# Top-k attention and a SoLU block in one kernel: score buffers over half of the keys for two heads, two query loads per step, and a new order

## The chip, the cores and the metric

The kernel runs on one core of one Trainium2 chip. The metric is the device time of one execution in microseconds. Before the change it is 1203.38 us, the median of three runs (1203.36 to 1203.61). Engines are named as in the profile: PE (TensorE), DVE (VectorE), ACT (ScalarE), POOL (GpSimd), and SP, which here issues all loads and stores.

## The reference

q, k and v have shape (8, 8, 576, 64): batch, heads, sequence, head size, in float32. The second block has float64 weights of 512 x 1024 and 1024 x 512.

```python
scores = scale * np.matmul(q, k.transpose(0, 1, 3, 2))
kth = np.partition(scores, -top_k, axis=-1)[..., -top_k:-top_k + 1]   # top_k = 32
scores = np.where(scores >= kth, scores, -1000000000.0)
scores = scores - np.max(scores, axis=-1, keepdims=True)
attn = np.exp(scores)
attn = attn / (np.sum(attn, axis=-1, keepdims=True) + 1e-09)
x = np.matmul(attn, v)            # then (B,H,S,D) -> (B*S, H*D): 4608 x 512
...
h = x @ w_in
e = np.exp(h - np.max(h, axis=-1, keepdims=True))
solu = h * (e / (np.sum(e, axis=-1, keepdims=True) + 1e-09))
ln = (solu - mean) / np.sqrt(var + 1e-06) * g_ln
out = ln @ w_out
```

So each query keeps its 32 largest of 576 scores, takes a softmax over them, and the result goes through two matrix products with a gate and a layer norm between them.

## The kernel before

**Tiling.** 576 queries are four blocks of 128 and a tail of 64. The work is in 32 *steps*, four for each batch: a step takes two pairs of heads and two blocks of queries of each, which makes four chunks of 128 queries x 2 heads, and a fifth chunk with the two tails of one pair. A score row block is called j: j = 2t and 2t+1 are the two heads of chunk t, j = 8 is the tail chunk. Steps 2n and 2n+1 of a batch together give the attention output of two blocks of 128 tokens for all heads; these are *tokens* (36 groups of 128 rows), and the second block runs once for each: mm1 (x w_in), hexp, solu, square, spread, ln, transpose_ln, mm2 (x w_out), store, send.

**A step.** SP loads q (load_q, L2125, four loads, one for each chunk) and, for each pair of heads, k, the tails of q and k, and v (load_k, load_t, load_v). PE turns them (prep_q, prep_k, prep_t; the rows tp_qk and pre); ACT copies them out and squares them. PE makes an estimate of each row's score size (estimate, the rows est), DVE's length and POOL's root turn it into a first threshold, which begin (L2184) puts into t0. PE then multiplies queries by keys: scores (L2202) handles one chunk t at a time. It takes two PSUM buffers `big` of 2 x 512 words, one for each head, with keys 0 to 287 in the first half and 288 to 575 in the second. A head has 64 rows, so the two heads use the upper and the lower half of the PE array, and their products stand alternately in the queue. ACT's evac (L2221) scales one buffer into X in SBUF, DVE counts how many of its scores pass t0 (count0, the rows junkv; two to four of the nine on ACT), moves the threshold by the count (second, moved, even), ACT counts again with signs (count1, the rows sg), DVE picks the values nearest to the threshold (nearest, best: the MAX8 rows), merges them into the exact 32nd value (merged, which, chosen, kth), and keeps the exponentials above it (keep, the rows E). PE turns these (transpose_p, transpose_last), ACT copies them into PT (copy_p), PE multiplies them by v (attn_v, attn_t, the rows om), and DVE's copy_v divides by the sums into xTm or xTt, which are the tokens' input.

**The weights.** Sixteen chunks of 512 KB are loaded as float64 (load_w), cut to float32 by DVE (w_bits, w_corr), added up on PE (w_sum) and copied by ACT (w_copy). mm1 needs all of w_in, so the first eight must be through. At the end they are loaded again and looked at (w_again, w_exp, w_check).

**Order.** All engines but SP follow an order written out by a planner. work_of lists each operation with its engine, an assumed duration, what it comes after, and which buffers it uses; PLACES holds one number, a due date, for each operation; arranged (L698) goes through time, and on each engine it takes, of the operations that can start soonest (within PATIENCE of the soonest, L1777), the one with the smallest place. SP's loads are issued in this order too. PE uses its array in three forms, the full one (`f`), by row halves (`r`, scores) and by column halves (`c`, attn_v), and the plan books a price for each change of form. Buffers that matter here: two `big` (scores, and mm1's result for a whole token), two `o` (estimates, attention outputs, mm2's results, turned tails), two `tp` (transposes), eight X.

Of the kernel before, what the change touches and what calls it, by code (L numbers as in the profile page):

```python
# [15 lines left out]
P = 128  # L16
# [426 lines left out]
class Work:  # L443
# [18 lines left out]
    "ends", "keep", "ln", "key_stats", "w_bits", "w_corr", "w_gain",  # L462
# [31 lines left out]
def work_of(B, NP, steps, NF, w_wide):  # L494
# [15 lines left out]
    for b in range(B):  # L510
        for hp in range(NP):
            n = pair(b, hp)
            add(("load_k", n), "SP", 1350, behind("load_k", n), [("km", n)], late=2300)
            add(("load_t", n), "SP", 1650, behind("load_t", n), [("qkt", n)], late=3000)
            add(("load_v", n), "SP", 1650, behind("load_v", n), [("vm", n), (f"vd{n % 4}", n)], late=3000)
# [9 lines left out]
    for i, (b, chunks) in enumerate(steps):  # L525
# [3 lines left out]
        add(("load_q", i), "SP", 2200, behind("load_q", i), [("q", i)], late=2400)  # L529
# [10 lines left out]
        add(("begin", i), "DVE", 80, [("root", i)], [("o", ("est", i)), ("small", i)], 80)  # L540
        turned = [("transpose_last", i - 1, u) for u in range(2)] if i else []
        turned += [("transpose_p", i - 1, j) for j in range(NT)] if i else []
        for t in range(NM + 1):
# [6 lines left out]
            add(("scores", i, t), "PE", 970, ready + [("scores", i - 1, u) for u in before],  # L550
                [("big", (i, j)) for j in js] + x + [("kT", n)] + ([("qT", i)] if t < NM else []),
                mode="r" if t < NM else "f")
            for j in js:
                add(("evac", i, j), "ACT", 531, [("scores", i, t)], [("big", (i, j)), ("small", i)] + x, 110)
                on_a = j >= NT - few_of(i)
                add(("count0", i, j), "ACT" if on_a else "DVE", 770 if on_a else 737,
                    [("begin", i), ("evac", i, j)], x + [("small", i)], 110 if on_a else 82)
# [103 lines left out]
    for n in range(NW):  # L661
        if w_wide:
            tag = ("X", ("w", n)) if 2 <= n < 6 else ("E", ("w", n)) if 6 <= n < 10 else ("lnT", ("w", n))
            add(("load_w", n), "SP", 2700, behind("load_w", n), [tag], 3500)
# [33 lines left out]
def arranged(work, rank):  # L698
# [23 lines left out]
    while len(start) < len(ops):  # L722
# [56 lines left out]
        -231922, -235093, -18042, -259815, 53881, -26910, 98693, 89295, 121016, 46316, 230106,  # L779
        355121, 274522, 360371, 391010, 446355, 444309, 504026, 537837, 507457, 575009, 582585,  # L780
        750366, 671489, 709965, 699022, 831359, 799848, 825482, 840407, 964227, 982302,
    ],
    "load_t": [
        -247901, -201100, -260957, 23891, 20177, 142488, 125581, 104238, 96313, 290803, 250948,
        316178, 307259, 403270, 342301, 413782, 396239, 494754, 589937, 526814, 579905, 664149,
        686757, 657519, 760755, 797410, 777584, 782250, 759984, 828408, 986254, 1052144,
    ],
    "load_v": [
        4513, -28316, 65834, 70032, 237412, 276299, 189136, 198676, 274775, 314238, 308304,
        315468, 396251, 396215, 501580, 466234, 545375, 599484, 587563, 603323, 638479, 756008,  # L790
        748529, 764396, 836844, 775398, 911922, 867656, 992809, 1068251, 1042268, 1092371,
    ],
    "prep_t": [
        -66024, -35218, -106968, -124979, 106380, 92968, 113423, 124982, 186474, 259308, 243381,
        264175, 349208, 365073, 403353, 423445, 427516, 433224, 489877, 478123, 625612, 662465,
        677716, 720421, 790096, 792821, 833195, 820447, 902635, 952541, 903717, 984623,
    ],
    "prep_tc": [
        -3659, 6982, 125129, 194480, 58479, 110962, 16603, 132387, 247838, 253849, 255570, 364359,
        401263, 437048, 412216, 468592, 538576, 465027, 572960, 574254, 624893, 670844, 740941,  # L800
        688304, 822521, 772593, 803972, 799637, 876671, 914493, 987945, 1053957,
    ],
    "prep_k": [
        -66034, -37947, -116787, -114223, 61830, 112826, 44679, 124730, 221869, 282666, 218678,
        312796, 373609, 360416, 374756, 444621, 506839, 560741, 514149, 602405, 665351, 668819,
        660569, 737807, 783550, 770963, 815648, 854771, 921629, 983616, 926036, 997868,
    ],
    "prep_kc": [
        -31830, 34481, -43910, 188250, 14844, 72034, 129236, 181508, 247818, 306656, 255884,
        418155, 369635, 416315, 460884, 487557, 508176, 499093, 549171, 549826, 679307, 654196,  # L810
        730255, 740546, 813255, 656582, 761008, 847058, 1011512, 968974, 1021267, 1014780,
    ],
    "key_square": [
        -6107, 9200, -18931, 213036, 67709, 48480, 69177, 125029, 263257, 285990, 199299, 423686,
        366563, 422347, 432668, 464275, 526013, 529993, 663289, 617129, 615223, 689260, 733195,
        763121, 824760, 755412, 803556, 820850, 972811, 973391, 963453, 1065640,
    ],
    "tail_square": [
        -9398, -37371, 24328, 181845, 66940, 136814, 56754, 125050, 274345, 247045, 271022,
        361521, 313475, 423910, 396880, 417393, 448163, 489613, 561645, 544046, 671031, 673625,  # L820
        718576, 687624, 812310, 696685, 804699, 833105, 852776, 972218, 965549, 1038215,
    ],
    "key_stats": [
        49244, 90323, 131224, 7666, 155042, 84463, 99397, 97289, 253693, 307081, 241289, 211979,
        339462, 399467, 402326, 455602, 486238, 511354, 589917, 612160, 565404, 712946, 729447,
        715533, 757814, 727456, 817143, 897941, 916106, 958459, 945063, 1071720,
    ],
    "load_q": [
        -203866, 57324, 47623, 69971, -30777, -6747, 92399, 81781, 190840, 208167, 261724, 303295,
        302878, 366925, 467745, 502581, 494867, 437968, 460600, 600618, 608413, 668795, 680197,  # L830
        761552, 682102, 671226, 845894, 865571, 874423, 860434, 1017679, 975249,
    ],
    "prep_q": [
        -79677, -117866, 32032, 13411, 86950, 135549, 225889, 127973, 183269, 276392, 244143,
        336055, 374788, 314311, 427218, 502907, 575463, 550697, 484754, 603196, 662484, 708755,
        710771, 750650, 762039, 831240, 855758, 847165, 910722, 955644, 1037349, 1050639,
    ],
    "prep_qc": [
        -2082, 188201, 134073, 119961, 51146, 125087, 198593, 145727, 249393, 219238, 284776,
        340139, 381991, 373070, 445301, 406892, 528101, 558348, 560625, 609324, 613546, 702436,  # L840
        680953, 773525, 758549, 795279, 864443, 884402, 902803, 974600, 1007236, 1087201,
    ],
    "query_square": [
        48602, 219690, 10502, 204666, 77178, 115847, 200979, 184149, 259522, 249591, 359749,
        338859, 430728, 461236, 461439, 480399, 516251, 557645, 605853, 636513, 639337, 685605,
        695232, 779265, 734075, 807377, 902692, 935429, 938819, 975439, 1117707, 1080921,
    ],
    "estimate": [
        -51721, 24520, 32537, 42039, 32686, 43251, 188650, 175963, 183605, 293926, 314412, 304383,
        406485, 355203, 465841, 523950, 454436, 555291, 600732, 655321, 676831, 585411, 743542,  # L850
        767341, 797214, 877957, 887133, 892412, 966830, 1025698, 881531, 1005532,
    ],
    "length": [
        13505, 24395, 62143, 74804, 27409, 136316, 213529, 202175, 282027, 342718, 372938, 330157,
        492709, 436992, 478114, 487587, 493364, 622122, 589139, 617588, 678258, 747400, 748131,
        761353, 821982, 912838, 922484, 921913, 987763, 1030027, 1037987, 1090530,
    ],
    "root": [
        119641, 113709, 124208, 125050, 115227, 123468, 183009, 143050, 342821, 318954, 283414,
        288875, 476686, 507680, 494982, 529348, 539265, 557472, 575475, 651531, 750654, 756244,  # L860
        740467, 755497, 809920, 900416, 886522, 961896, 980436, 1024386, 979437, 1047371,
    ],
    "begin": [
        -11098, -32177, 114058, 97689, 127135, 163126, 183911, 238625, 258237, 332322, 343785,
        337307, 443545, 446760, 512382, 463995, 468265, 527542, 611248, 597194, 702846, 746359,
        777678, 796090, 780698, 866074, 840375, 898381, 996092, 1006714, 1032142, 1052602,
    ],
    "scores": [
        [-66043, -32432, -117187, -55548, -58649],
        [32509, -86744, -84674, 14425, -118098],  # L870
        [-1709, 59539, 206, 62497, 1680],
        [97632, 36717, 37420, 110204, 21187],
        [126461, 66992, 95602, 22391, 180659],
        [225092, 132274, 170298, 187038, 132279],
        [221524, 185438, 98417, 149447, 208257],
        [235554, 234327, 205686, 276399, 197567],
        [274165, 278537, 273676, 258560, 301244],
        [278510, 351700, 329880, 301926, 326114],
        [326121, 301381, 291542, 293719, 437364],
        [320084, 368685, 363929, 372753, 342271],  # L880
        [363314, 353920, 356109, 316998, 390713],
        [283384, 427244, 513881, 447027, 282054],
        [589195, 496452, 535821, 356932, 465873],
        [517528, 510229, 487313, 458650, 439441],
        [553852, 547378, 551693, 443165, 441345],
        [564875, 622931, 590176, 557220, 582546],
# [1854 lines left out]
```

## Time and profile before

| What | us |
|---|---|
| Median of three runs | 1203.38 |
| The profiled execution, its own time | 1203.71 |
| Its span, first to last instruction | 1201.9 |
| PE busy, mean granted clock 0.982 | 1147.5 |
| s_ps, row-half products (1024 rows, 512 products) | 170.1 busy |
| h_ps and o_ps, products with w_in and w_out | 229.2 + 28.9 and 257.9 busy |
| sg on ACT, second counts | 196.5 busy |
| root on POOL (zs, 32 times) | 1.976 each |

One product in float32 appears as two rows in the profile, a transpose as one. Times are starts and durations from the span's beginning; ends on PE are modelled, so the distance from one start to the next says more than a duration. The profile's page gives the engines' totals and a strip of 40 slices of 30 us each, in tenths. The timeline merges rows of one kind that follow each other, with the idle time before them and what ended it in brackets.

### The profile page before, as it was taken

Reading aid. Unit: us, or ns where it says so; the run is one execution under the profiler, and the core shown is the slowest. Engines: PE = TensorE matmul, PEld = TensorE weight load, DVE = VectorE, ACT = ScalarE, POOL = GpSimd, SP = SyncE. Lnnn points to the kernel's source line nnn. Section 1 sums busy time; section 2 is a strip of 40 time slices with the busy share of each in tenths; the row PEclk is TensorE's granted clock in tenths of the full one; section 3 lists DMA queues with packets and bytes.
Section 4 is the critical chain, followed back from the end, with each engine's and each line's share of the span. In section 5 each row is a group of like instructions: output and inputs, shape, how many; then the busy total and the mean of one; then the engine's idle time right before and its main releaser. Section 6 shows DMA issues by size and latency. Waiting matters only on the chain.

```text
span 1201.9 us, 18981 instructions
## 1 busy us (share of the span) xinstructions
PE 1147.5 (95%) x5866; PEld 661.0 (55%) x5868; DVE 1047.0 (87%) x3113; ACT 1011.2 (84%) x2180; POOL 149.9 (12%) x167
## 2 busy tenths in 40 slices
PE   6676999999999999999999999999999999999997
PEld 3354555555655655565565555555555556555553
DVE  5899899999888998999989888999898888999910
ACT  7789779989987998999896999899887899888642
POOL 1100020202022020210012020211113001110110
PEclk9689899999999999999999999999999999999999
DMA  6312201111110211120120211111120011122501
GB/s 174 113 53 71 88 21 52 35 31 42 58 47 18 60 43 56 30 69 24 39 66 10 52 44 51 49 36 46 31 74 28 25 28 41 57 71 90 177 19 30
DMA packets 111433, 64.56 MB, mean 54 GB/s; under 512 B 90445, under 2 KB 98906, under 8 KB 111322
## 3 DMA queue, kind: packets, MB, share of 16 engines
q1 hardware_dynamic: 111322, 63.25, 18.8%
q8 instruction: 49, 0.80, 0.3%
q14 instruction: 62, 0.51, 0.1%
HBM read 53.65 MB, written 9.57 MB: 53 GB/s over the span
## 4 chain that ended last, share of the span: by engine, by line
PE 58%; DVE 23%; ACT 14%; issue 2%; POOL 1%; DMA 1%; SPq 0%; DVEq 0%; ACTq 0%
PE o_ps L2625 16%; PE h_ps L2564 11%; PE s_ps L2214 10%; PE tp_p L2467 7%; PE om L2523 7%; DVE junkv L2231 5%; ACT sg L2288 4%; DVE w L2320 4%; DVE w L2309 4%; DVE E L2390 4%; ACT E L2345 2%; PE tp_ln L2614 2%; PE tp_qk L2087 2%; PE om L2532 2%; ACT PT L2480 2%
## 5 line engine op out<-in xcount | busy, mean ns | idle before, releaser
L2625 PE MATMUL o_ps<-w_out,lnT 128*128 128x512 f32 x576 | 257.9, 593 | 0.1
L2564 PE MATMUL h_ps<-w_in,xTm 128*128 128x512 f32 x512 | 229.2, 594 | 0.0
L2320 DVE MAX8 w<-w 128x8 f32<-128x288 f32 x576 | 224.1, 446 | 0.3
L2288 ACT ACTIVATE sg<-X,t 128x576 bf16<-128x576 f32 x256 | 196.5, 778 | 12.6 <-DVE t L2273 12.1
L2309 DVE SCALAR_TENSOR_TENSOR w<-X,al,sg 128x576 f32<-128x576 f32 x256 | 202.0, 815 | 0.9
L2390 DVE SCALAR_TENSOR_TENSOR E<-X,kth,E 128x576 f32<-128x576 f32 x256 | 198.6, 816 | 2.3 <-ACT E L2345 1.1
L2223 ACT ACTIVATE X<-s_ps 128x576 f32<-128x576 f32 x256 | 159.1, 664 | 41.9 <-PE s_ps L2214 41.1
L2231 DVE TENSOR_SCALAR_CACHE_REDUCE junkv<-X,t 128x576 bf16<-128x576 f32 x216 | 174.4, 807 | 13.4 <-ACT X L2223 7.0
L2214 PE MATMUL s_ps<-kT,qT 64*128 64x288 f32 x1024 | 170.1, 440 | 1.6 <-ACT X L2223 0.8
L2467 PE MATMUL tp_p<-ident,E 128*128 128x128 f32 x1024 | 151.3, 279 | 17.8 <-ACT PT L2480 6.2
L2625 PEld LDWEIGHTS o_ps<-w_out,lnT 128*128 128x128 f32 x576 | 105.1, 190 | 111.1 <-issue 110.3
L2480 ACT COPY PT<-tp_p 128x512 f32<-128x512 f32 x256 | 148.0, 598 | 13.1 <-PE tp_p L2467 12.8
L2467 PEld LDWEIGHTS tp_p<-ident,E 128*128 128x128 f32 x1024 | 116.0, 141 | 77.8 <-issue 29.9
L2345 ACT ACTIVATE E<-X 128x1152 f32<-128x1152 f32 x128 | 149.6, 1187 | 0.9 <-PE tp_p L2467 0.9
L2564 PEld LDWEIGHTS h_ps<-w_in,xTm 128*128 128x128 f32 x512 | 93.3, 190 | 98.4 <-issue 96.3
L2523 PE MATMUL om<-PT,vm 128*64 128x256 f32 (+1 forms) x1024 | 138.5, 415 | 2.5 <-ACT PT L2480 1.5
L2182 POOL TENSOR_TENSOR zs<-zs,phalf 128x9 f32<-128x9 f32 x32 | 63.2, 1976 | 507.2 <-DVE zs L2175 500.0
L2214 PEld LDWEIGHTS s_ps<-kT,qT 64*128 64x128 f32 x1024 | 96.7, 191 | 52.8 <-issue 24.2
L2523 PEld LDWEIGHTS om<-PT,vm 128*64 128x64 f32 x1024 | 69.5, 138 | 58.5 <-issue 10.4
L2599 POOL TENSOR_SCALAR var<-var 128x1 f32<-128x1 f32 x36 | 12.7, 354 | 514.3 <-ACT e_sb L2593 514.2
L2593 ACT ACTIVATE e_sb<-solu,nmu 128x1024 f32<-128x1024 f32 x36 | 41.5, 1152 | 14.8 <-DVE nmu L2587 14.6
L2575 ACT ACTIVATE e_sb<-h_ps 128x1024 f32<-128x1024 f32 x36 | 36.7, 1020 | 19.9 <-PE h_ps L2564 19.8
(144 smaller groups left out, 1506.9 us busy)
## 6 DMA issues: line engine op xcount, KB each, us to landing
km<-in_k_dram SPq DMA_DIRECT2D x32, 256.0 KB
q_sb<-in_q_dram SPq DMA_DIRECT2D x128, 64.0 KB
vm<-in_v_dram SPq DMA_DIRECT2D x32, 256.0 KB
out_dram<-osb SPq DMA_DIRECT2D x32, 256.0 KB
scales<-rows SPq DMA_DIRECT2D x58, 128.0 KB
w_raw<-in_moe_w_in_dram SPq DMA_DIRECT2D x8, 512.0 KB
w_raw<-in_moe_w_out_dram SPq DMA_DIRECT2D x8, 512.0 KB
w_again<-in_moe_w_in_dram SPq DMA_DIRECT2D x8, 512.0 KB
```

The costliest lines, as they stand in the source:

```text
L2214: nc.tensor.matmul(out=big[h][:, half, 0:SH], lhsT=queries_of(i, t)[hd, :], rhs=kT[hd, k0 : k0 + SH], start=True, stop=True,)
L2231: nc.vector.tensor_scalar(out=junk, in0=x_of(i, j), scalar1=st[i][t][:, j : j + 1], scalar2=None, op0=ALU.is_ge, op1=ALU.add, accum_out=co ...
L2288: nc.scalar.activation(out=d["sg", j], in_=x_of(i, j), func=AF.Sign, scale=-(1.0 + 2.0**-23), bias=d["t1"][:, j : j + 1], accum_out=column ...
L2309: nc.vector.scalar_tensor_tensor(out=w, in0=x_of(i, j), scalar=d["al"][:, j : j + 1], in1=d.pop(("sg", j)), op0=ALU.subtract, op1=ALU.mult,)
L2320: nc.vector.max(w8[:, j, 8 * half : 8 * half + 8], w[:, half * SH : (half + 1) * SH])
L2345: nc.scalar.activation(out=d["E", t], in_=d["X", t], func=AF.Exp)
L2390: nc.vector.scalar_tensor_tensor(out=e, in0=x_of(i, j), scalar=d["kth"][:, j : j + 1], in1=e, op0=ALU.is_ge, op1=ALU.mult, accum_out=den_a ...
L2467: nc.tensor.transpose(tp[:, c, :], e[:, c * P : (c + 1) * P], ident)
L2480: nc.scalar.copy(out=dst, in_=st[i].pop(("tp", j)))
L2523: nc.tensor.matmul(out=o[h * D : (h + 1) * D, cols], lhsT=vm[:, h, c, :], rhs=pt[:, h * NM + c, :], start=(c == 0), stop=False,)
L2564: nc.tensor.matmul(out=h[:, half, :], lhsT=x[:, c, :], rhs=w_in[:, c, half * 512 : (half + 1) * 512], start=(c == 0), stop=(c == NP - 1),)
L2625: nc.tensor.matmul(out=o, lhsT=d["lnT"][:, c, :], rhs=w_out[:, c, :], start=(c == 0), stop=(c == NF - 1),)
```

## The change

1. **Scores by halves of the keys.** The operation is now scores(i, j). For chunk t it takes one buffer `big`; the first 512 words hold head 0 and the second 512 words head 1, both for the same 288 keys. j = 2t is the first half of the keys, 2t+1 the second. evac writes the two heads' parts into the two rows' places in X. A first count of a head now comes after both evictions of its chunk. The tail chunk stays as it was.
2. **Queries in two loads.** A step's four chunks are two neighbouring pairs of heads at two neighbouring blocks, so one load fetches four heads of one block. The tile's axes change, and the turning picks its four parts from it.
3. **Estimates leave PSUM at once.** length scales both halves of the estimate with a constant tile `parts` into SBUF; begin adds them from there and no longer holds the estimate's PSUM buffer.
4. **ranks** is one row of 16 constants, read by broadcast over the nine j.
5. **The plan.** Other assumed durations for loads, PATIENCE above zero, and new PLACES for all operations.

```diff
-            add(("load_k", n), "SP", 1350, behind("load_k", n), [("km", n)], late=2300)
-            add(("load_t", n), "SP", 1650, behind("load_t", n), [("qkt", n)], late=3000)
+            add(("load_k", n), "SP", 950, behind("load_k", n), [("km", n)], late=2300)
+            add(("load_t", n), "SP", 1800, behind("load_t", n), [("qkt", n)], late=2100)
...
-        add(("begin", i), "DVE", 80, [("root", i)], [("o", ("est", i)), ("small", i)], 80)
+        add(("begin", i), "DVE", 80, [("root", i)], [("small", i)], 80)
...
-            add(("scores", i, t), "PE", 970, ready + [("scores", i - 1, u) for u in before],
-                [("big", (i, j)) for j in js] + x + [("kT", n)] + ([("qT", i)] if t < NM else []),
-                mode="r" if t < NM else "f")
             for j in js:
-                add(("evac", i, j), "ACT", 531, [("scores", i, t)], [("big", (i, j)), ("small", i)] + x, 110)
+                add(("scores", i, j), "PE", 485 if t < NM else 970,
+                    ready + [("scores", i - 1, u) for u in range(NT if i else 0)],
+                    [("big", (i, j))] + x + [("kT", n)] + ([("qT", i)] if t < NM else []),
+                    mode="r" if t < NM else "f")
+                add(("evac", i, j), "ACT", 531, [("scores", i, j)], [("big", (i, j)), ("small", i)] + x, 110)
+            for j in js:
                 on_a = j >= NT - few_of(i)
                 add(("count0", i, j), "ACT" if on_a else "DVE", 770 if on_a else 737,
-                    [("begin", i), ("evac", i, j)], x + [("small", i)], 110 if on_a else 82)
+                    [("begin", i)] + [("evac", i, u) for u in js], x + [("small", i)], 110 if on_a else 82)
...
-PATIENCE = {"PE": 0, "ACT": 0, "DVE": 0, "POOL": 0, "SP": 0}
+PATIENCE = {"PE": 300, "ACT": 100, "DVE": 100, "POOL": 100, "SP": 2000}
...
     def load_q(i):
         b, chunks = steps[i]
-        qt = st[i]["q"] = p2.tile([P, 2 * NM, D], F32, tag="q", name="q_sb")
-        for c, (hp, t) in enumerate(chunks):
-            nc.sync.dma_start(
-                out=qt[:, 2 * c : 2 * c + 2, :],
-                in_=q[b, 2 * hp : 2 * hp + 2, 0:SM, :].rearrange("h (p t) d -> p t h d", t=NM)[
-                    :, t, :, :
-                ],
-            )
+        first, t = min(chunks)
+        qt = st[i]["q"] = p2.tile([P, 2, NM, D], F32, tag="q", name="q_sb")
+        rows = q[b, 2 * first : 2 * first + NM, 0:SM, :].rearrange("h (p t) d -> p t h d", t=NM)
+        for n in range(2):
+            nc.sync.dma_start(out=qt[:, n, :, :], in_=rows[:, t + n, :, :])
...
     def length(i):
-        zs = st[i]["zs"] = small.tile([P, NT], F32, tag="zs", name="zs")
-        nc.vector.tensor_scalar(
-            out=zs, in0=st[i]["est"][:, 0, 0:NT], scalar1=(Z0 * scale) ** 2 / SM, scalar2=None,
-            op0=ALU.mult,
-        )
+        both = st[i]["both"] = small.tile([P, 2, NT], F32, tag="zs", name="zs")
+        st[i]["zs"] = both[:, 0, :]
+        nc.vector.tensor_tensor(
+            out=both, in0=st[i]["est"][:, :, 0:NT], in1=parts, op=ALU.mult
+        )
...
-    def scores(i, t):
+    def scores(i, j):
         d = st[i]
+        t, k = divmod(j, 2)
         kT = keys_of(i, t)["kT"]
-        js = [2 * t] if t == NM else [2 * t, 2 * t + 1]
-        big = [ps_big.tile([P, 2, 512], F32, tag="big", name="s_ps") for _ in js]
-        for half in range(2):
-            for h in range(len(js)):
-                hd = slice(0, P) if t == NM else slice(h * D, (h + 1) * D)
-                k0 = half * SH + (ST if h == 0 else 0)
-                nc.tensor.matmul(
-                    out=big[h][:, half, 0:SH], lhsT=queries_of(i, t)[hd, :],
-                    rhs=kT[hd, k0 : k0 + SH], start=True, stop=True,
-                )
-        for j, s in zip(js, big):
-            d["s", j] = s
+        s = d["s", j] = ps_big.tile([P, 2, 512], F32, tag="big", name="s_ps")
+        for n in range(2):
+            if t == NM:
+                hd, k0 = slice(0, P), ST + n * SH
+            else:
+                hd, k0 = slice(n * D, (n + 1) * D), k * SH + (ST if n == 0 else 0)
+            nc.tensor.matmul(
+                out=s[:, n, 0:SH], lhsT=queries_of(i, t)[hd, :],
+                rhs=kT[hd, k0 : k0 + SH], start=True, stop=True,
+            )
     def evac(i, j):
-        d = st[i]
+        t, k = divmod(j, 2)
+        if t == NM:
+            x = x_of(i, j).rearrange("p (a s) -> p a s", a=2)
+        else:
+            x = x2_of(i, t).rearrange("p (h s) -> p h s", h=2)[:, :, k * SH : (k + 1) * SH]
         nc.scalar.activation(
-            out=x_of(i, j).rearrange("p (a s) -> p a s", a=2), in_=d.pop(("s", j))[:, :, 0:SH],
-            func=AF.Copy, scale=scale,
+            out=x, in_=st[i].pop(("s", j))[:, :, 0:SH], func=AF.Copy, scale=scale,
         )
```

How the new places order the engines, by the instruction orders of the two built kernels: SP begins with k of pair 0, its tails, q of step 0 and k of pair 1, and issues the first weight chunk fifth; before, the first weight chunk went first. DVE finishes step 1 before it begins the first counts of step 2; before, counts of steps 2 and 3 stood among step 1's work. PE changes its array form 347 times rather than 317, and visits the row form 145 times rather than 127; 98 of these visits hold two halves, 42 one, 5 three or four.

## The prediction

> **What bounds the kernel now.** I read engine totals and slices first, then engine time by stage, then the timelines of DVE and PE at the two places where those point. The page:
>
> ```profile
> PE 1147.5 (95%) x5866; PEld 661.0 (55%) x5868; DVE 1047.0 (87%) x3113; ACT 1011.2 (84%) x2180; POOL 149.9 (12%) x167
> PE   6676999999999999999999999999999999999997
> DVE  5899899999888998999989888999898888999910
> PEclk9689899999999999999999999999999999999999
> ```
>
> PE has little room anywhere but in the first four or five slices, where its clock is also held back. By stage (columns: stretch, length, then busy time of PE, weight loads, DVE, ACT, POOL, granted clock, DMA share, GB/s):
>
> ```profile
> 0.00:40.00 40.00, 23.78 (x96) 14.24 (x98) 24.03 (x66) 32.34 (x79) 3.29 (x28) 0.85 0.69 185
> 40.00:80.00 40.00, 29.27 (x159) 17.35 (x157) 34.35 (x100) 30.64 (x66) 3.60 (x2) 0.77 0.17 51
> 80.00:120.00 40.00, 30.67 (x185) 18.93 (x181) 37.97 (x111) 37.52 (x91) 2.23 (x1) 0.96 0.28 73
> 120.00:140.00 20.00, 18.50 (x108) 11.58 (x109) 16.88 (x57) 15.99 (x38) 1.83 (x1) 0.83 0.28 80
> 140.00:200.00 60.00, 59.58 (x289) 32.83 (x290) 57.62 (x155) 46.08 (x93) 7.00 (x7) 1.00 0.15 47
> 300.00:1150.00 850.00, 842.34 (x4406) 488.31 (x4405) 772.84 (x2305) 743.06 (x1588) 110.72 (x104) 1.00 0.18 51
> ```
>
> PE idles 38 us of the first 140 and 1 to 2% later, apart from 7 us after the last product. So **two regimes**: a fill, in which DVE's top-k work of the first steps releases PE's work, and a long stretch at PE's rate. Nothing after 140 us can give more than the 10 us that PE still idles there; the fill can give up to 38. What sets the fill on DVE:
>
> ```profile
> 18.27 0.17 DVE L2175 TENSOR_SCALAR zs<-est 128x9 f32<-128x9 f32 x1 [0.38 <-PE est L2168]
> 20.46 0.17 DVE L2187 SCALAR_TENSOR_TENSOR t<-est,zs 128x9 f32<-128x9 f32 x1 [2.02 <-POOL zs L2182]
> ...
> 45.85 0.17 DVE L2175 TENSOR_SCALAR zs<-est 128x9 f32<-128x9 f32 x1 [2.70 <-PE est L2168]
> ...
> 203.52 0.42 DVE L2546 TENSOR_TENSOR xTm<-om,scales 128x256 f32<-128x256 f32 x1
> ```
>
> Counting starts at 20.46, when the first estimate has passed PE, DVE and POOL. DVE stalls again for step 1's estimate at 45.85. The last row is step 3's copy into xTm; the third token's first product starts 0.33 us behind it:
>
> ```profile
> 135.77 0.38 PE L2467 MATMUL tp_p<-ident,E 128*128 128x128 f32 x2
> 136.08 1.24 PE L2214 MATMUL s_ps<-kT,qT 64*128 64x288 f32 x8
> 137.25 1.09 PE L2467 MATMUL tp_p<-ident,E 128*128 128x128 f32 x8
> ...
> 203.85 2.41 PE L2564 MATMUL h_ps<-w_in,xTm 128*128 128x512 f32 x5
> ```
>
> **The start (load_q, transposed, places of steps 0 and 1).** The changed queue issues k of pair 0, its tails, the two q loads, k of pair 1, and only then weights; now a 512 KB weight load goes first and q takes four issues (2.23 us from 3.79). At the rows' issue times (k 0.63, three tail loads 1.9, q 0.57 each) k goes out at 0.72, tails at 1.4, q at 3.3, the second k at 4.5. Now k takes 3.5 us from issue (3.12) to use (6.61): it lands at 4.2, and ACT starts at 4.7, behind four transposes. ACT's work before estimate 0, at its starts' spacing: two key pairs at 1.18, two tail groups at 0.47, five evictions at 0.53, qT 0.48, Et's exponential 0.58, query square 0.51: 7.5 us, and 1.1 us of waiting for the second k (8.0): 13.3. Estimate and length bring 14.1; POOL's root takes 1.98, and DVE has one weight pair (2.4) in front of begin: **16.6 us against 20.46, so 3.9 us**. Ahead of begin DVE holds the same work in both, so this shifts DVE's whole fill. The other way round, if q lands late, this falls to nothing; bounds 0 and 5.
>
> **DVE's order in the fill.** I added up, in the instruction order of both built kernels, what DVE holds ahead of an instruction, at the spacing of starts in long runs (count 0.74, nearest 0.73, a pair of MAX8 0.72, keep 0.745, a weight pair 2.4, merge stage 0.29, small ones 0.08 to 0.22). Ahead of step 1's last copy: 113.5 us before, 94.9 after; the changed order finishes step 1 before it counts for later ones. Ahead of step 3's: 176.0 before, 171.7 after (four counts, four merges, one which fewer: 2.96+1.16+0.22). So tokens 0 and 1 reach PE about 19 us of DVE work earlier, but the third only 4.3. The early pair can fill PE with 4 x 6.9 us of mm1 and mm2, which is then missing later: what counts is the later edge. Ahead of the third token PE's set of operations is identical.
>
> **DVE's stalls.** Between 20.46 and 203.52 DVE has 183.1 us for 170.9 of work: 12.1 idle. Of that 2.7 us is estimate 1's row; the changed queue issues q for step 1 at about 10 us instead of 19.7 to 26.1, so I take 2 off; bounds: 6 off and 4 more, because every first count (DVE) now waits for both evictions of its pair, one 0.53 us eviction per pair, sixteen pairs in four steps, 8.5 us at worst. In step 0 I followed it: the first pair is out by 12 us, ahead of begin, so I price it at zero; if ACT falls behind, that cover goes.
>
> **Scores by halves of the keys.** The same 512 row-half products and evictions; one buffer at a time rather than two. Removed: waiting for two free buffers. PE's whole wait there in front of products is 1.6 us (page, s_ps row), so I count no gain. Added: PE changes its array form more often. A group of four row-half products takes 1.17 us (136.08 to 137.25) where two full-array ones of 288 columns take 0.97 (middle spacing over 150 to 1150 us); two transposes in front of it take 0.31 instead of 0.22; four behind it 0.49 instead of 0.44. So a visit costs 0.20+0.09+0.05, about **0.35 us**. In the orders, visits to the row form go from 127 to 145 and all changes of form from 317 to 347; 98 pairs of halves still stand together. The Trainium skill, "TensorEngine Tiling (Array Packing)", Key Properties, says that each change of mode drains the engine. Taken as a rule it speaks against cutting the operation: 256 lone halves would be 129 more visits, 45 us. The order gives 18 more, 6.3 us, and 22 of the 30 extra changes lie ahead of the third token, where PE idles. On the path: 8 changes, 1.4 us. The same page (PSUM Pressure) wants different banks under the two row halves. Before, the two heads write two buffers; now the two 512-word halves of one. "PSUM — Partial Sum Buffer", Specifications, gives 512 fp32 words a bank, so they stay apart; no row of before shows two heads in one buffer. If they did collide, pairs would run one after the other, 128 x 0.97 = 124 us. I take zero.
>
> The eviction writes two runs of 288 in separate places instead of 576 in a row. Nearest rows: PT written in four strided blocks costs 598 ns, lnT in one piece 599. Zero; bounds 0 and 2 us in the fill.
>
> **Small edits.** length now reads both estimates and begin none: est's buffer goes free at length, not at begin. Two 0.16 us rows stay two; products waiting for begin are 0.6 us: at most 1 us won, zero taken. ranks by broadcast: `which` keeps its 0.30 us; POOL's sixteen fills and two more precede its first root by 10 us. In steady work SP loses two issues a step, 1.1 us of a queue that nobody on the path waits for.
>
> **The sum.** Third token: 3.9 + 4.3 + 2 = 10.2 earlier, less 1.4. But step 5 asks for the 4.3 back: DVE work through a keep plus PE work from there on peaks at 1143.5 before (209 us of DVE work) and 1142.2 after (217), changes of form included. At that edge the gain is 1.3 + 3.9 + 2, plus what DVE no longer stalls for a late PE there (it idles 1 us more between 176 and 209): **8 us**. Profiled: 1201.9 - 8 = 1194 span; its own execution took 1203.71, the median of runs is 1203.38, so 1.5 us stand around the span: **1195**.
>
> **Rivals.** What a measurement tells from no change is 0.2%, 2.4 us.
> - *The forecast*, 4 to 13 us less, 1190 to 1199: **0.62**.
> - *The fill fully opened*: the first product at 140.4 comes 19 us of DVE work earlier, plus 4, and the third token does not starve because DVE's 12 us of stalls mostly go. Gain 13 to 20: 1184 to 1190. For it: ACT's work through step 1's last copy falls from 97.2 to 80.5 us. Against: step 5's edge. **0.14**.
> - *The early gain is handed back*: DVE's order from step 2 to 5 is as full as before, second estimates wait as long; 1201 to 1204, within 2.4 us or a little better: **0.12** (0.07 of it within 0.2%).
> - *Slower: changes of form.* PE's stretch from 140 to 1190 us has no cover; 18 more visits at 0.35 are 6.3 us, and the lone halves bring waits for their evictions. It decides once the fill brings less than 4 us: then 1206 to 1210. Against: most extra visits are early. **0.12**.
>
> Faster by over 0.2% 0.81, within 0.07, slower 0.12. For 8 in 10 the range reaches into the second and the third case: 1187 to 1204.
>
> **What would show it.** Right: begin of step 0 near 16.6 us; DVE's second stall for est gone or shorter; the first h_ps product near 115 to 122 us; the third token's near 194; PE idle in 0 to 140 smaller; four row-half products still 1.17 us, transposes 0.44. Wrong: s_ps groups of four near 2 us (banks); begin at 19 or later; PE idle back between 150 and 250 us (handed back); PE busy higher by 5 us in the middle (changes of form).

## The result, and the profile after

The changed kernel takes **1193.57 us** (median of 6 runs, 1193.13 to 1196.47) where the kernel before, run beside it, takes 1203.49 (1202.88 to 1203.88). The ratio is 0.9922, with a 95% interval of 0.9909 to 0.9935: 9.9 us less. Predicted were 1195 with a range of 1187 to 1204, and 8 us of gain. The total was right; two of its terms were not.

The profiled execution took 1193.35 us, its span is 1191.5. From its page, the engine totals and the strip of slices:

```profile
PE 1143.5 (96%) x5868; PEld 648.2 (54%) x5868; DVE 1054.0 (88%) x3113; ACT 1014.4 (85%) x2180; POOL 154.4 (13%) x169
PE   6689999999999999999999999999999999999997
DVE  4999999999899999899979998899989888999821
PEclk9799999999999999999999999999999999999999
```

PE's slices are full from the fourth on; before, from the fifth. By stage (stretch, length, busy time of PE, weight loads, DVE, ACT, POOL, then granted clock, DMA share, GB/s):

```profile
0.00:40.00 40.00, 25.44 (x96) 13.86 (x96) 23.61 (x65) 31.28 (x72) 3.39 (x30) 0.87 0.68 181
40.00:80.00 40.00, 29.93 (x208) 17.94 (x209) 38.15 (x113) 35.34 (x81) 3.67 (x2) 0.91 0.27 72
80.00:120.00 40.00, 35.79 (x199) 18.80 (x196) 38.65 (x107) 38.54 (x87) 3.67 (x2) 1.00 0.32 94
120.00:140.00 20.00, 18.71 (x61) 8.90 (x60) 19.65 (x61) 11.95 (x29) 2.13 (x3) 1.00 0.15 43
140.00:200.00 60.00, 58.27 (x342) 33.83 (x341) 59.71 (x181) 52.37 (x109) 5.66 (x5) 1.00 0.17 48
300.00:1150.00 850.00, 843.33 (x4364) 482.56 (x4361) 772.14 (x2285) 736.04 (x1571) 115.89 (x104) 1.00 0.18 50
```

Set these beside the same rows of before. From 300 to 1150 us nothing moved: PE 843.3 against 842.3. The gain is in the first 140 us, where DVE is busy for 120.1 us rather than 113.2, and PE for 109.9 rather than 102.2. The clock differs too: the stretches at half of the full clock, added up in the trace, last 41 us between 20 and 127 us before, and 17 us after (26.4 to 33.3, 36.7 to 40.1, 53.7 to 60.6). That is not what the gain needs: coarse_tuned (run 9) has 34 us of them and is as fast.

The start, and the edge that the prediction named, in the timelines of DVE, PE and ACT (start, duration, engine, line, operation; in brackets the idle time before and what ended it):

```profile
17.33 0.18 DVE L2180 TENSOR_TENSOR zs<-est,parts 128x18 f32<-128x18 f32 x1 [2.64 <-PE est L2172]
19.68 0.16 DVE L2191 TENSOR_TENSOR t<-zs 128x9 f32<-128x9 f32 x1
...
189.92 0.42 DVE L2549 TENSOR_TENSOR xTm<-om,scales 128x256 f32<-128x256 f32 x1
```

```profile
6.88 2.29 PE L2216 MATMUL s_ps<-kT,qTt 128*128 128x288 f32 x4 [1.08 <-ACT qTt L2082]
...
10.80 3.71 PE L2216 MATMUL s_ps<-kT,qT 64*128 64x288 f32 x16
14.44 0.44 PE L2076 MATMUL pre<-ident,qk_tails 128*128 128x128 f32 x2
14.87 2.02 PE L2216 MATMUL s_ps<-kT,qT 64*128 64x288 f32 x8
...
144.80 1.24 PE L2216 MATMUL s_ps<-kT,qT 64*128 64x288 f32 x8
145.97 0.66 PE L2470 MATMUL tp_p<-ident,Et 128*128 128x128 f32 x4
...
185.98 0.76 PE L2216 MATMUL s_ps<-kT,qT 64*128 64x288 f32 x4
186.67 2.48 PE L2526 MATMUL om<-PT,vm 128*64 128x320 f32 x16
...
190.99 3.60 PE L2567 MATMUL h_ps<-w_in,xTm 128*128 128x512 f32 x8
```

```profile
5.40 0.60 ACT L2110 ACTIVATE junka<-tp_qk 128x512 bf16<-128x512 f32 x1 [3.40 <-PE tp_qk L2092]
...
9.20 0.65 ACT L2227 ACTIVATE Xt<-s_ps 128x576 f32<-128x576 f32 x1 [2.03 <-PE s_ps L2216]
```

Step 0's begin starts at 19.68, not at 16.6. The first s_ps group takes 2.29 us here and 1.21 before: PE still runs at half clock, until 12.8 us in this trace, and ACT waits 2.03 us for that group. (The trace's record of the clock begins at 12.8 us; the rows of the table above count what lies before it as full. That it was half is read from PE's rows.) The last s_ps group ahead of the estimate stands behind the transposes of pair 1's tails, which come at 14.44. All the same the third token's first product starts 12.9 us earlier than before (203.85). A half of the keys (185.98 to 186.67) takes 0.69 us, and two halves together 1.17 (144.80 to 145.97), as two buffers did before: the two heads' rows in one buffer do not collide.

DVE's waits in the first 150 us (which operation waited for what: us in total, times, longest):

```profile
DVE stats L2121 <- ACT kT L2103: 10.2, 2, 5.4
DVE zs L2180 <- PE est L2172: 3.1, 2, 2.6
```

Nearly all of these two lies ahead of step 0's begin. From begin to step 3's copy DVE needs 170.2 us for 166.6 us of work: 3.7 idle, where before it was 12.1. (Counted as gaps in the traces it is 6.3 and 14.8; the difference is the same.)

Where the runs below stand in the fill, read from their timelines (begin on DVE, h_ps on PE, in us; the last column is the span less the fifth token):

| kernel | begin | first h_ps | third token | fifth token | span | rest |
|---|---|---|---|---|---|---|
| before | 20.5 | 140.4 | 203.9 | 270.6 | 1201.9 | 931.3 |
| changed | 19.7 | 114.6 | 191.0 | 259.3 | 1191.5 | 932.2 |
| four_q_loads | 19.1 | 116.2 | 191.9 | 260.2 | 1192.0 | 931.8 |
| warm | 20.2 | 116.8 | 193.2 | 261.5 | 1194.0 | 932.5 |
| dve_early | 19.8 | 120.7 | 197.0 | 265.3 | 1197.5 | 932.2 |
| dve_mid | 19.3 | 116.5 | 192.8 | 261.1 | 1200.7 | 939.6 |
| form_row | 19.8 | 116.7 | 193.8 | 263.5 | 1208.4 | 944.9 |
| form_full | 19.9 | 116.0 | 193.5 | 263.4 | 1218.2 | 954.8 |
| coarse_tuned | 18.1 | 120.1 | 194.8 | 260.4 | 1191.7 | 931.3 |
| old_code_tuned | 18.3 | 119.3 | 198.5 | 264.6 | 1197.9 | 933.3 |
| before_tuned | 20.8 | 135.2 | 201.6 | 268.7 | 1198.4 | 929.7 |
| after_tuned | 18.3 | 114.3 | 191.7 | 258.9 | 1193.6 | 934.7 |

Where nothing was added behind it, the fifth token is followed by 930 to 935 us whatever the kernel. The change moved the fifth token 11.3 us forward and the end 10.4. A difference of less than about 2 us in this table tells nothing: dve_mid carries out the changed kernel's own instructions up to 565 us, and its fifth token is 1.8 us later, with 24 us at half clock in the fill rather than 17.

### The profile page after: what moved, and what is told of

The parts are those of the page before. It is cut to its first block, busy times and chain, and to the rows that moved or that the text cites. A ratio compares the mean times of both kernels' runs of the same rounds, so it can differ in the third digit from the quotient of the medians.

```text
span 1191.5 us, 18863 instructions
## 1 busy us (share of the span) xinstructions
PE 1143.5 (96%) x5868; PEld 648.2 (54%) x5868; DVE 1054.0 (88%) x3113; ACT 1014.4 (85%) x2180; POOL 154.4 (13%) x169
## 3 DMA queue, kind: packets, MB, share of 16 engines
q1 hardware_dynamic: 110298, 63.25, 18.8%
## 4 chain that ended last, share of the span: by engine, by line
PE 50%; DVE 27%; ACT 17%; issue 3%; POOL 2%; DMA 0%; DVEq 0%; ACTq 0%; POOLq 0%
PE o_ps L2628 14%; PE h_ps L2567 9%; PE s_ps L2216 9%; ACT sg L2291 7%; PE tp_p L2470 6%; PE om L2526 6%; DVE junkv L2234 6%; DVE w L2323 5%; DVE w L2312 5%; DVE E L2393 3%; ACT PT L2483 2%; DVE solu L2586 2%; ACT X L2227 2%; PE tp_ln L2617 2%; PE om L2535 2%
## 5 line engine op out<-in xcount | busy, mean ns | idle before, releaser
L2526 PE MATMUL om<-PT,vm 128*64 128x320 f32 (+1 forms) x1024 | 136.1, 411 | 1.0 <-ACT osb L2635 0.9
L2216 PEld LDWEIGHTS s_ps<-kT,qT 64*128 64x128 f32 x1024 | 85.7, 186 | 68.3 <-issue 22.2
L2578 ACT ACTIVATE e_sb<-h_ps 128x1024 f32<-128x1024 f32 x36 | 36.7, 1020 | 20.0 <-PE h_ps L2567 19.7
```

Of the source, the lines that this page charges most:

```text
L2216: nc.tensor.matmul(out=s[:, n, 0:SH], lhsT=queries_of(i, t)[hd, :], rhs=kT[hd, k0 : k0 + SH], start=True, stop=True,)
L2526: nc.tensor.matmul(out=o[h * D : (h + 1) * D, cols], lhsT=vm[:, h, c, :], rhs=pt[:, h * NM + c, :], start=(c == 0), stop=False,)
```

## The experiments

The theory: the order of the first steps on DVE makes the gain, and halves of scores and paired loads are worth little. The main rival: the halves are what lets the first steps go early.

**1 and 2. Plan and operations crossed.** The places of one kernel were put onto the operations of the other; a score operation takes the earlier place of its halves.

```diff
 # old_code_new_plan: the kernel before with
-PATIENCE = {"PE": 0, "ACT": 0, "DVE": 0, "POOL": 0, "SP": 0}
+PATIENCE = {"PE": 300, "ACT": 100, "DVE": 100, "POOL": 100, "SP": 2000}
-            add(("load_k", n), "SP", 1350, behind("load_k", n), [("km", n)], late=2300)
+            add(("load_k", n), "SP", 950, behind("load_k", n), [("km", n)], late=2300)
...
 PLACES = {
...
```

> The code of before (scores of a whole chunk in two buffers, four query loads, begin reading PSUM) under the changed kernel's places, patience and load durations; a chunk's scores take the smaller place of its two halves. Theory 'order' (DVE finishes step 1 first, keys and queries go before weights): most of the 10 us comes with the plan alone, 1193 to 1197 us, DVE idle between begin and step 3's copy stays near 4 us. Rival 'buffers' (single buffers remove the stalls of the fill): the plan alone brings 0 to 3 us, 1200 to 1204 us, DVE idle back at 10 us or more.

> The changed code under the places, patience and load durations of before; both halves of a chunk take the chunk's old place. Theory 'order': the fill is as before, 1200 to 1206 us. Rival 'buffers': 1193 to 1198 us. If both this and the run with the old code are near 1203, the two need each other.

Measured: 1318.18 us (ratio 1.0955, 1.0940 to 1.0971) and 1401.42 (1.1638, 1.1622 to 1.1654). Both expectations failed. In the first, the span grows by 112 us and PE's busy time by only 37 (1184.0 of 1314.0); DVE and ACT stall all through the run. From its waits:

```profile
DVE al L1852 <- ACT sg L1843: 70.2, 30, 4.8
...
ACT X L1778 <- PE s_ps L1769: 53.3, 52, 3.0
```

DVE waits 30 times for counts on ACT, and ACT 52 times for scores: a list of due dates is fitted to the very operations that it was made for. Crossing them says nothing of which part gains. Runs 9 to 12 put the question again, with plans fitted to each.

**3. Query loads in four again.** The changed kernel, each of the two loads cut in two, same places.

```diff
-            nc.sync.dma_start(out=qt[:, n, :, :], in_=rows[:, t + n, :, :])
+            for hp in range(2):
+                nc.sync.dma_start(
+                    out=qt[:, n, 2 * hp : 2 * hp + 2, :],
+                    in_=rows[:, t + n, 2 * hp : 2 * hp + 2, :],
+                )
```

> The changed kernel with each step's queries in four loads again, in the same places of the queue. Theory 'order': two issues of 0.57 us more in front of the second pair's keys delay the first estimate by about 1.1 us and the end by as much or less, 1193.5 to 1195 us. Rival 'the two loads matter': the queue is short of time in the whole fill, the second estimates come late, 1197 us or more.

Measured: 1194.62 us (1193.84 to 1196.18), ratio 0.9922 (0.9909 to 0.9936), the same ratio as the changed kernel's; begin at 19.12, no later than in the changed kernel. Two issues fewer a step bring nothing that these runs can tell.

**4. PE at full clock from the start.** Six products of a tile of zeros go ahead of everything on PE.

```diff
+        warm = ps_tp.tile([P, NM, P], F32, tag="tp", name="warm")
+        for n in range(6):
+            nc.tensor.matmul(
+                out=warm[:, n % NM, :], lhsT=v_diag[3], rhs=v_diag[3], start=True, stop=True
+            )
```

> The changed kernel with six products of a zero tile on PE ahead of its work (from about 2 us on), their result unused. In the changed kernel's trace PE works at half clock until 12.8 us, and begin of step 0 comes at 19.7 instead of 16.6 us. Theory 'the half clock held the first estimate back': begin moves to 17 to 18.5 us and the end by the same 1 to 2.5 us, 1191 to 1192.5 us. Rival 'the first estimate waits for ACT or loads': begin stays within 0.5 us of 19.7, or is later by what the products take, 1193.5 to 1195 us.

Measured: 1194.61 us (1193.79 to 1195.80), ratio 0.9918 (0.9905 to 0.9932): no gain. From PE's timeline of this run (the profiled execution was the slowest of the five):

```profile
7.01 1.24 PE L2216 MATMUL s_ps<-kT,qTt 128*128 128x288 f32 x4 [1.29 <-ACT qTt L2082]
...
9.47 1.24 PE L2216 MATMUL s_ps<-kT,qT 64*128 64x288 f32 x8 [0.26 <-ACT qT L2154]
11.18 1.30 PE L2216 MATMUL s_ps<-kT,qT 64*128 64x288 f32 x8 [0.47 <-ACT X L2227]
14.02 0.46 PE L2076 MATMUL pre<-ident,qk_tails 128*128 128x128 f32 x2 [1.55 <-DMA qk_tails<-in_q_dram]
14.41 2.95 PE L2216 MATMUL s_ps<-kT,qT 64*128 64x288 f32 x8
```

The groups do run at full speed (1.24 rather than 2.29 us), and then PE waits 1.55 us for the tails of pair 1, loaded behind two weight chunks; after 15.3 us the clock is half again, and the last group takes 2.95 us. Begin comes at 20.17. So the slow clock alone did not hold the first estimate: the load of the tails stood right behind it, and the clock that came early was lost again before the estimate.

**5 and 6. What a visit to the row form costs.** One small product of two columns ahead of each second half, 128 in all; with the full array it can part two halves that stood together, with the row half it doesn't. The score products themselves follow and overwrite its two columns.

```diff
+        if k == 1:
+            nc.tensor.matmul(   # form_full
+                out=s[:, 0, 0:2], lhsT=ident, rhs=ident[:, 0:2], start=True, stop=True
+            )
...
+            nc.tensor.matmul(   # form_row
+                out=s[:, 0, 0:2], lhsT=queries_of(i, t)[0:D, :], rhs=kT[0:D, 0:2],
+                start=True, stop=True,
+            )
```

> The changed kernel in its own order, with one more product on PE in front of each second half of a chunk's scores (128 in all): full array, two columns, into the buffer that the scores then overwrite; its value is not used. It parts most of the 98 visits to the row form that hold two halves. Theory 'a visit costs 0.35 us on a PE without cover': about 110 more visits, of which some 15 in the fill are covered, so 33 us plus what the small products themselves cost (see form_row): 1220 to 1240 us. Rival 'changes of form are hidden': within 3 us of form_row.

> As form_full, but the small product uses the upper row half, as the scores do: the same number of products, no change of form. Both theories: 128 products at 0.05 to 0.15 us, 1197 to 1213 us. The difference of form_full to this is the price of the changes of form.

Measured: form_full 1220.88 us (ratio 1.0147, 1.0130 to 1.0163), form_row 1210.69 (1.0061, 1.0044 to 1.0077). PE's timeline of form_full around one parted pair:

```profile
509.16 0.38 PE L2212 MATMUL s_ps<-ident 128*128 128x2 f32 x2
509.47 0.76 PE L2220 MATMUL s_ps<-kT,qT 64*128 64x288 f32 x4
510.16 0.38 PE L2212 MATMUL s_ps<-ident 128*128 128x2 f32 x2
510.47 0.76 PE L2220 MATMUL s_ps<-kT,qT 64*128 64x288 f32 x4
```

Two lone halves take 2 x 0.69 us where a pair takes 1.17. The two runs differ by 10.2 us for 50 more visits (195 and 145 by their traces; 110 more were expected): **0.20 us each** at the kernel's end, and 0.15 to 0.26 by the intervals of the two ratios. On PE itself a visit costs more. From the last row of the first half, past the small product, to the row behind the second half, the median over the 44 parted places between 150 and 1080 us is 1.33 us in form_full and 1.03 in form_row: 0.30 more. So the prediction's 0.35 is nearly what the rows show, and a part of it is covered. The small products that part nothing differ between the two runs as well (by 0.1 us less to 0.3 more in form_full), so 0.20 is a rough price.

**7 and 8. The same delay on DVE, early and late.** Seven extra counts into a scratch tile (expected as 5.2 us; from start to start they take 5.6 in both traces), ahead of the first count of step 0 or of step 16.

```diff
+        if (i, j) == (0, 1):      # dve_mid: (16, 1)
+            for _ in range(7):
+                junk = p1.tile([P, S], BF16, tag="junkv", name="junkv")
+                nc.vector.tensor_scalar(
+                    out=junk, in0=x_of(i, j), scalar1=0.0, scalar2=None,
+                    op0=ALU.is_ge, op1=ALU.add, accum_out=columns(i, "idle")[:, 0:1],
+                )
```

> The changed kernel in its own order, with seven more counts (0.74 us each, 5.2 us, result unused) on DVE in front of the first count of step 0. Theory 'DVE's work in the fill sets when PE's long stretch begins': the end moves by 4 to 5.5 us, 1197.5 to 1199 us. Rival 'PE alone limits': DVE catches up, 0 to 1.5 us, 1193.5 to 1195 us.

> The same seven counts in front of the first count of step 16 instead. Both theories have PE as the limit there: 0 to 1.5 us, 1193.5 to 1195 us. If it costs 4 us or more as well, DVE is on the path everywhere, and the split into a fill on DVE and a stretch on PE falls.

Measured: early 1198.95 us (ratio 0.9955, 0.9938 to 0.9971), 5.4 over the changed kernel by the medians and 4.0 by the two ratios, as the theory has it; PE's products of the first token (120.7 rather than 114.6) are already late by the delay, and it stays to the end. Late 1202.14 (1200.26 to 1202.63; 0.9981, 0.9973 to 0.9989), 8.6 over it by the medians and 7.1 by the ratios. Here the theory failed: PE was not covered. PE's timeline of dve_mid, then the changed kernel's rows at that place, then dve_mid's stage from 578.2 to 585 us (columns as above):

```profile
573.67 1.88 PE L2635 MATMUL o_ps<-w_out,lnT 128*128 128x512 f32 x4
580.35 1.94 PE L2477 MATMUL tp_p<-ident,E 128*128 128x128 f32 x8 [4.79 <-DVE E L2400]
582.08 5.02 PE L2635 MATMUL o_ps<-w_out,lnT 128*128 128x512 f32 x8
```

The same E and the same transposes in the changed kernel, where PE does not wait:

```profile
572.18 0.81 DVE L2393 SCALAR_TENSOR_TENSOR E<-X,kth,E 128x576 f32<-128x576 f32 x1
573.54 1.04 PE L2470 MATMUL tp_p<-ident,E 128*128 128x128 f32 x8
```

```profile
578.20:585.00 6.80, 4.65 (x12) 3.08 (x13) 6.80 (x28) 5.54 (x14) 0.00 (x0) 0.50 0.00 0
```

PE waits 4.79 us for DVE's E, the clock falls to a half for 6.8 us, and PE's starts, 1.9 us behind the changed kernel's up to 570 us, are 9.0 us behind from there to the end. So the added work cost 7.2 us; the other 1.9 were there before it. In the changed kernel this E ends at 572.99 and PE takes it at 573.54: in a fixed order DVE can be as little as 0.6 us ahead of PE in the middle too.

**9 to 12. Plans fitted to each set of operations.** For these four the places were searched for anew, with the planner's own durations: by small moves of due dates, keeping what shortens the planned time.

```diff
 # coarse_tuned: the changed kernel with
-                add(("scores", i, j), "PE", 485 if t < NM else 970,
...
+            add(("scores", i, t), "PE", 970, ready + [("scores", i - 1, u) for u in before],
+                [("big", (i, j)) for j in js] + x + [("kT", n)] + ([("qT", i)] if t < NM else []),
...
-                    [("begin", i)] + [("evac", i, u) for u in js], x + [("small", i)], 110 if on_a else 82)
+                    [("begin", i), ("evac", i, j)], x + [("small", i)], 110 if on_a else 82)
...
-    def scores(i, j):
+    def scores(i, t):
...
 PLACES = {
...
```

The functions scores and evac are those of before in it. In old_code_tuned all code is that of before, under the load durations and PATIENCE of run 1; before_tuned and after_tuned differ from before and changed in PLACES alone.

> The changed kernel with one thing undone: a score buffer again holds all keys of one head, both heads' buffers are taken at once. Everything else is as changed, and the places are searched for anew from the changed order. Theory (halves are worth nothing, their 18 visits to row form cost a little): 1188 to 1196. Rival (one buffer at a time is what lets the first steps go early): 1199 or more.

> All code of the kernel before (two score buffers per pair of products, four q loads per step, the counts as they were), but with places searched for anew from the changed kernel's order of the work, so that the plan fits these operations. Theory (what helped is the order of the first steps; halves of scores and loads in pairs are worth less than a few us): time within 5 us of the changed kernel's 1193.6, that is 1189 to 1199; first h_ps product before 122 us. Rival (the order needs the one-buffer scores): above 1199, near the 1203.9 of the kernel before, with PE waiting for score buffers.

> The kernel before, its places improved by the same search, but from its own order of the work. It shows what the search alone brings. Theory: most of what there is to gain lies in another order of the first steps, which small moves from the old order reach only in part: 1196 to 1203. Rival (the search is what gains, whatever order it starts from): as fast as the other searched kernels, within 2 us of them.

> The changed kernel with its places searched for further from its own order. Theory (PE is busy 96% of the span, and 20 us of DVE's lag lie in the start): little is left, 1188 to 1193. Rival (durations assumed by the plan no longer resolve such differences): 1192 to 1197, no better than the changed kernel.

Measured, against 1203.54 us for the kernel before in the same series:

| kernel | median us | lowest to highest | ratio | 95% interval |
|---|---|---|---|---|
| coarse_tuned | 1191.52 | 1189.34 to 1193.54 | 0.9895 | 0.9880 to 0.9910 |
| old_code_tuned | 1199.06 | 1198.10 to 1201.99 | 0.9965 | 0.9953 to 0.9978 |
| before_tuned | 1199.60 | 1198.06 to 1200.21 | 0.9964 | 0.9950 to 0.9977 |
| after_tuned | 1196.29 | 1195.37 to 1196.97 | 0.9941 | 0.9927 to 0.9954 |

*The halves are not needed.* With two score buffers a chunk again, and a plan that fits, the kernel is at least as fast as the changed one; it is the fastest of all the runs, though its interval touches the changed kernel's. Its stages and PE's timeline show the fill:

```profile
40.00:80.00 40.00, 32.41 (x165) 19.97 (x167) 34.60 (x101) 31.04 (x69) 4.12 (x2) 0.66 0.20 53
...
80.00:120.00 40.00, 35.22 (x234) 20.69 (x232) 37.26 (x108) 38.32 (x88) 4.10 (x2) 1.00 0.29 83
```

```profile
257.13 1.95 PE L2456 MATMUL om<-PT,vm 128*64 128x256 f32 x16
...
260.41 1.88 PE L2497 MATMUL h_ps<-w_in,xTm 128*128 128x512 f32 x4
```

The fifth token starts 10.2 us before that of the kernel before, even with a clock of 0.66 between 40 and 80 us. It gets there another way than the changed kernel: begin comes 2.4 us earlier (18.1), and up to step 3's copy DVE idles 12.5 us, counted as gaps, hardly less than before (14.8).

*The order alone brings a part.* old_code_tuned reaches 1199.06, at the boundary of what the two theories expected: its first h_ps comes at 119.3, as the theory has it, but the fifth token only 6 us earlier than before. A search from the old order reaches the same time (1199.60). That a new order is needed for these 4 us is thus not shown. The two gain in different places, though: at the fifth token the new order is 6.0 us ahead, the search from the old one 1.9, and the latter makes up the rest behind it (929.7 rather than 933.3). So the new order moves the fill, but about half of the 11.3 us there came without the other edits.

*What the rest is stays open.* Between old_code_tuned and coarse_tuned lie 7.5 us and these edits: q in two loads, length and begin on a copy, the small `ranks`. The loads alone cost nothing in run 3, under a plan made for them. The search itself also misses by some us: after_tuned, expected at 1193 or less, came out 2.7 us slower than the kernel it started from. So these runs don't tell the small edits from a luckier plan.

## Why the prediction was right, and where it was not

- **What bounds the kernel.** "Two regimes", a fill set by DVE and a long stretch at PE's rate: the first half holds (the fifth token moved by 11.3 us and the end by 10.4; a delay in the fill passes whole, run 7). The second half, taken as "DVE has room there", falls: in run 8 a delay of DVE in the middle costs more than its own length.
- **The start, 3.9 us.** Mis-sized: it measured 0.8 (20.46 to 19.68), and the prediction's own sign of being wrong, begin at 19 or later, came true. The step that failed is the list of ACT's work up to estimate 0, which took PE's rows at full clock. ACT starts at 5.40 rather than 4.7, and it waits 2.8 us rather than 1.1, of which 2.03 for the first s_ps group at half clock; the full clock came only at 12.8 us. The row zs starts at 17.33, not 14.1. Of pair 1's loads the prediction followed k but not the tails, which stand behind two weight chunks. In the changed kernel no row waits for them; in run 4, with the clock mended, PE does, for 1.55 us.
- **DVE's order, 4.3 us at the third token.** The work ahead of step 3's last copy fell as counted in the orders, from about 171 us behind begin to 166.6.
- **DVE's stalls, 2 us.** Mis-sized the other way: idle time between begin and that copy fell from 12.1 to 3.7, so 8.4 us. The prediction took off one row, estimate 1's, which did fall from 2.70 to 0.47, and held the others fixed. The lag of DVE, its time less the work ahead of an instruction in the order, shows where they went: before, it grows from 15.7 us at the first count to 27.9 at 176 us of work; after, from 15.0 to 18.8 at 172. That finishing step 1 first left other work in front of each wait is argued from the orders; no run took out single stalls, and coarse_tuned gains as much with most of its stalls left.
- **The later edge.** Right in kind: 12.9 us at the third token, 11.3 at the fifth, 10.4 at the end. At 209 us of DVE work the lag is 20.1 against 28.9, but more work stands ahead there, so not all arrives.
- **Changes of form, 1.4 us.** Small, as forecast. The price of 0.35 us a visit is nearly what PE's rows show (0.30); 0.20 of it reached the end (runs 5 and 6). Of the 18 more visits in the trace (127 and 145), 13 lie ahead of the fifth token. The 5 behind it (96 and 101) would be 1.0 us at that rate, and that stretch is 0.9 us longer (931.3 and 932.2). The rival slower by 6.3 us took all 18 as uncovered. The rule that the prediction took from the Trainium skill, "TensorEngine Tiling (Array Packing)", Key Properties, that a change of mode drains the array, fits these rows: parted halves cost 1.38 us rather than 1.17. The drain itself no row shows.
- **Banks, strided evictions, small edits: zero.** Four row-half products still take 1.17 us. The loads are zero by run 3, as far as 2 us can be told. The others were only tested together, and there stand the 7.5 us that are open.

The errors of two terms, 3.1 us too much and 6.4 too little, cancel in part: 8 was forecast and 9.9 came. That the total came so close is in part luck.

## What to carry to other kernels

Where engines run a fixed list, look for the instant in the fill after which everything follows at a nearly constant distance (here the fifth token, 930 to 935 us before the end), and price a change by what it does to that instant. A change to operations and the plan that was fitted with it can't be judged apart by crossing them; fit a plan to each, and know how far such fits miss (here one came out 3 us worse). And when working out a start, follow every load on the way to the first result, the last and smallest among them too, and price PE's first products at the clock that they get.

## What the runs showed of the hardware

- **The clock in the middle of a run.** In run 8 one wait of 4.79 us on PE, from 575.55 us, brought 6.8 us at a granted clock of 0.50, from 578.1 on. The Trainium skill, "TensorE: Matmul & The Clock Gate", What's actually happening, says that an idle window of about 3.4 us throttles the array to half. The run agrees in kind, but the clock fell sooner, after 2.6 us of waiting. The price on a full PE: 5.6 us of added work on DVE cost PE 7.2 us from there on.
- **Half clock comes in pieces of 3.41 us.** In all fourteen traces each stretch at half clock ahead of 1150 us lasts a whole multiple of 3.41 us: 3.4, 6.8, 10.2, 13.7, 17.1 or 20.5.
- **Warm once is not warm for good.** In run 4 the full clock came at 5.1 us and was gone at 15.3, after a stretch with several short waits, the longest 1.55 us. No wait of 3.4 us stands before it, so the rule above does not cover this fall; what in that stretch set it off no run took apart.
- **Two heads in one PSUM buffer.** Their row-half products, in the two 512-word halves, run side by side at 1.17 us for four, the same as in two buffers.
